# Six blocks of 384 tokens in place of one of 256 and four of 512, in a linear-attention, SwiGLU and ELU kernel

## The chip, the cores and the metric

The kernel runs on one core of one Trainium2 chip. The metric is the device time of one execution in microseconds (us). A change counts as faster or slower when it moves the time by more than 0.2%, which is about what a measurement of this kernel can tell from no change.

Four compute engines matter here: TensorE (PE in the rows; PEld is its loading of weights), VectorE (DVE), ScalarE (ACT) and GpSimd (POOL). SyncE (SP) issues the DMAs.

## The reference

Shapes: four batches, 8 heads, 576 positions, head size 64, hence 2304 tokens of model size 512; hidden sizes 1536 and 2048. The weights are float64, everything else float32.

```python
kv = np.einsum('bhsd,bhse->bhde', k, v)
out = np.einsum('bhsd,bhde->bhse', q, kv)
x = out / np.sqrt(np.mean(out * out, axis=-1, keepdims=True) + 1e-06) * g_norm
# heads side by side: x is [2304, 512]
xn = x / np.sqrt(np.mean(x * x, axis=-1, keepdims=True) + 1e-06) * rms_g
g = xn @ w_gate
x = g * (1.0 / (1.0 + np.exp(-g))) * (xn @ w_val) @ w_out
h = x @ w_in2
y = np.where(h > 0.0, h, np.exp(np.minimum(h, 0.0)) - 1.0) @ w_out2
```

## The kernel before

The 2304 tokens are 18 tiles of 128. The attention part goes by tiles: `sum_kv` makes a batch's k-by-v sums on TensorE, `attend` multiplies a tile's q with them (tile `po`), `norm` does the two norms on DVE, ACT and POOL (tiles `x`, `ms`, `me`, `ri`), and `turn` transposes the tile on TensorE (tile `pt`) and splits it exactly into two float32r parts, `xh` (copy on ACT) and `xl` (subtraction on DVE).

From there the work goes by **token blocks**. A block's tokens are the moving operand of the big products; `blocks` holds one of two tiles (256 tokens, block 0) and four of four tiles (512 tokens). x lies transposed, with the model dimension on the partitions, as two parts `xh` and `xl` for each block. Each weight chunk of 128x128 is also kept as two parts (`h...`, `l...`), and a product of weight and x is three matmuls, lines 240 to 242: high by high, high part of the weight by low part of x, low part of the weight by high part of x. So each 128x128 piece of a weight is used in three matmuls per block, whatever the block's size, and the moving operand has 512 or 256 columns.

The hidden dimension goes in chunks of 128, two chunks to a **group** (`G = 2`). There are six groups in the first phase (`hidden1`: gate `pg`, value `pv`, SiLU, product) and eight in the second (`hidden2`: `ph`, ELU). For one block in a group of the first phase, TensorE runs 48 matmuls for the two chunks' `pg` and `pv` and 24 for `back` (`pb`, the product with the output weights, added on DVE to the block's sums `acc`, line 298): 72. In the second phase it is 24 for `ph` and 24 for `back`: 48. After each block's hidden products the loop runs the `back` of the block before it, and then `bring`, which loads and splits one weight of the next group (float64 to two float32r parts, lines 224 to 235, on DVE and ACT, in the first group with POOL's help). Block 0 brings none, blocks 1 to 3 bring one each, and the last block of the turn brings what is left: three of six in the first phase, one of four in the second.

At the start the loads of k, v and the first of q go to places that later belong to the sums and to later blocks' x (`homes`). Then come the first block's attention, the second block's, the first block's first products, and from there the attention of the other tiles runs ahead of the products of the first group, as `until_turned` says. The program's lines give priorities; a scheduler sets the order on each engine when the kernel is built, and the engines then run that order, each waiting for the others by semaphores. In the last group the blocks go 1, 2, 3, 4, 0, so block 0 is also the last to be written out.

Of the kernel before, what the change touches and what calls it, by code (L numbers as in the profile page):

```python
# [18 lines left out]
G = 2  # hidden chunks that one pass over the tokens takes  # L19
EPS = 1e-06  # L20
INF_FIELD = 2.0**-96 * 1.875  # as bits: float64's infinity of float32, its exponent rebiased
# [3 lines left out]
def linear_attention__swiglu__elu_kernel(  # L25
    ctx: ExitStack,
    tc: tile.TileContext,
    q: bass.AP,  # [two token tiles, head pair's dim, tile, pair, token]
    kv: bass.AP,  # [token tile, token, k or v, model dim]
    g_norm: bass.AP,  # [1, D]  # L30
    w_gate: bass.AP,  # float64: [hidden chunk, model dim in chunk, chunk, hidden dim]
    w_val: bass.AP,
    w_out: bass.AP,  # float64: [hidden chunk, hidden dim, model dim]
    rms_g: bass.AP,  # [1, model dim]
    w_in2: bass.AP,
    w_out2: bass.AP,
    out: bass.AP,  # [model dim in chunk, chunk, token]
# [9 lines left out]
    # token blocks: the moving operand of the products  # L47
    blocks = []
    at = 0
    while at < NT:  # L50
        n = min(4, NT - at) if at else (NT % 4 or 4)
        blocks.append((at, n))
        at += n
    NMAX = 4 * P
    block_of = {i: (t, i - a) for t, (a, n) in enumerate(blocks) for i in range(a, a + n)}

    # per partition: x as two parts 72 KiB, the sums 36, the weights as two parts 40, the rest below 8 to 16 each
# [26 lines left out]
    kv_sb = {}  # L84
    kv_blocks = [const.tile([P, KD, P], F32, name=f"kv{j}") for j in range(3)]
    for t in kv_blocks:
        nc.gpsimd.memset(t, 0.0)  # off the diagonal it stays zero: a head's q meets its own kv alone
    in_sb, q_sb = {}, {}
    # k, v and the first of q wait where the sums, and later blocks' x, will lie
    homes = {}  # L90
    for tag, n, what in (
# [3 lines left out]
    ):  # L95
        for j, x in enumerate(what):
            homes[x] = tag, n, j
# [14 lines left out]
    def sum_kv(b):  # L112
# [3 lines left out]
        for i in tiles:  # L116
            r0, r1 = max(lo - i * P, 0), min(hi - i * P, P)
            for p in range(KD):
                # one zeroing of the bank: the pairs' sums lie side by side in it
# [26 lines left out]
    def attend(i):  # L146
        """q @ kv of a token tile, and each head's 1/rms"""
# [21 lines left out]
    def norm(i):  # L169
        """the two norms of a token tile"""  # L170
# [18 lines left out]
    def new_x(t):  # L189
        n = blocks[t][1] * P  # L190
        xh[t] = res.tile([P, KD, n], F32R, tag=f"xh{t}", name=f"xh{t}")
        xl[t] = res.tile([P, KD, n], F32R, tag=f"xl{t}", name=f"xl{t}")
# [19 lines left out]
    def split(src, kind, name, bufs, other=None):  # L212
# [9 lines left out]
        # the high word's exponent from bias 1023 to 127 (as a float, its exponent counts eights),  # L222
        # at most infinity's, then sign, exponent and 20 bits into a float32's places
# [4 lines left out]
        # plus the low word at its weight, rounded once to float32  # L228
# [56 lines left out]
    def back(ws, acts, t, first, last, name, done):  # L285
        """acts @ ws onto the block's sums"""
# [26 lines left out]
    def units(phase, g):  # L313
        """A group's weights: calls that load and split one each, in the order of need."""
# [26 lines left out]
    # The loads, in the order of need. The first block's x waits for all of its batch's k and v.  # L341
# [14 lines left out]
    load_kv(3)  # L356

    # The first block, the second one's attention, the other batches' kv; GpSimd takes a share of
    # the weights' passes while the vector engine has the tokens' as well.
    coming = [coming[i] for i in (0, 1, 3, 4, 2, 5)]  # L360
    bring(2)
    sum_kv(0)
# [99 lines left out]
```

## Time and profile before

| | |
|---|---|
| device time, median of 3 | 922.0 us (921.58 to 922.02) |
| span of the profiled execution | 920.5 us |
| PE busy | 894.7 us, 97% of the span |
| DVE busy | 641.0 us, 70% |
| ACT busy | 309.6 us, 34% |
| POOL busy | 86.9 us, 9% |

The profiled execution gives its span, from the first to the last instruction; the median lies 1.5 us above it, for what lies around the span. Busy time of PE is a share of time in which a matmul is under way; matmuls overlap one another, so the distance from one start to the next is what a matmul costs on a full engine, and this is read from the timeline.

### The profile page before, as it was taken

Reading aid. Unit: us, or ns where it says so; the run is one execution under the profiler, and the core shown is the slowest. Engines: PE = TensorE matmul, PEld = TensorE weight load, DVE = VectorE, ACT = ScalarE, POOL = GpSimd, SP = SyncE. Lnnn points to the kernel's source line nnn. Section 1 sums busy time; section 2 is a strip of 40 time slices with the busy share of each in tenths; the row PEclk is TensorE's granted clock in tenths of the full one; section 3 lists DMA queues with packets and bytes.
Section 4 is the critical chain, followed back from the end, with each engine's and each line's share of the span. In section 5 each row is a group of like instructions: output and inputs, shape, how many; then the busy total and the mean of one; then the engine's idle time right before and its main releaser. Section 6 shows DMA issues by size and latency. Waiting matters only on the chain.

```text
span 920.5 us, 11272 instructions
## 1 busy us (share of the span) xinstructions
PE 894.7 (97%) x4472; PEld 760.4 (83%) x4472; DVE 641.0 (70%) x1162; ACT 309.6 (34%) x563; POOL 86.9 (9%) x104
## 2 busy tenths in 40 slices
PE   5799999999999999999999999999999999999998
PEld 5787788888888888888888888888888888888886
DVE  4979846558557556665776775787878787878644
ACT  1345543222212221221233565433433433433332
POOL 1757723000000000000000000000000000000000
PEclk9899999999999999999999999999999999999999
DMA  9812201012002010210210011110101110100023
GB/s 336 352 58 90 69 23 69 23 47 69 23 24 69 33 36 23 69 46 24 69 40 29 24 46 46 47 46 23 68 24 46 46 47 24 69 23 1 0 92 115
DMA packets 16725, 55.55 MB, mean 60 GB/s; under 512 B 1872, under 2 KB 2384, under 8 KB 16672
## 3 DMA queue, kind: packets, MB, share of 16 engines
q1 hardware_dynamic: 16560, 54.53, 16.5%
q8 instruction: 35, 0.57, 0.2%
q0 software_dynamic: 112, 0.30, 0.2%
q14 instruction: 18, 0.15, 0.1%
HBM read 50.10 MB, written 4.72 MB: 60 GB/s over the span
## 4 chain that ended last, share of the span: by engine, by line
PE 89%; DVE 4%; POOL 4%; issue 1%; DMA 1%; ACT 0%; SPq 0%; DVEq 0%; POOLq 0%
PE pb L240 12%; PE pb L241 12%; PE pb L242 12%; PE ph L241 7%; PE ph L242 7%; PE ph L240 7%; PE pg L240 5%; PE pg L241 5%; PE pg L242 5%; PE pv L240 5%; PE pv L242 5%; PE pv L241 5%; POOL ri L166 1%; DMA wxh<-in_kv 1%; PE kv L120 1%
## 5 line engine op out<-in xcount | busy, mean ns | idle before, releaser
L298 DVE TENSOR_TENSOR acc<-acc,pb 128x512 f32<-128x512 f32 (+1 forms) x240 | 146.9, 628 | 27.4 <-PE pb L242 25.7
L255 ACT ACTIVATE ah<-a 128x512 fp32r<-128x512 f32 (+1 forms) x140 | 82.4, 588 | 247.4 <-PE pb L242 115.6
L241 PE MATMUL ph<-xl,hi 128*128 128x512 f32 (+1 forms) x320 | 117.8, 368 | 0.0
L240 PE MATMUL ph<-xh,hi 128*128 128x512 f32 (+1 forms) x320 | 117.7, 368 | 0.0
L242 PE MATMUL ph<-xh,li 128*128 128x512 f32 (+1 forms) x320 | 117.7, 368 | 0.0
L269 DVE TENSOR_TENSOR a<-s,pv 128x512 f32<-128x512 f32 (+1 forms) x60 | 37.9, 632 | 113.9 <-PE pv L242 111.7
L241 PE MATMUL pb<-al,hp 128*128 128x512 f32 (+1 forms) x320 | 116.6, 368 | 0.0
L242 PE MATMUL pb<-ah,lp 128*128 128x512 f32 (+1 forms) x320 | 116.6, 368 | 0.0
L240 PE MATMUL pb<-ah,hp 128*128 128x512 f32 (+1 forms) x320 | 113.7, 368 | 0.0
L256 DVE TENSOR_TENSOR al<-a,ah 128x512 fp32r<-128x512 f32 (+1 forms) x140 | 90.1, 644 | 32.9 <-ACT ah L255 32.3
L240 PE MATMUL pg<-xh,hg 128*128 128x512 f32 (+1 forms) x240 | 88.7, 370 | 1.5 <-ACT xh L203 1.5
L241 PE MATMUL pg<-xl,hg 128*128 128x512 f32 (+1 forms) x240 | 88.8, 370 | 0.5 <-DVE xl L204 0.5
L240 PE MATMUL pv<-xh,hv 128*128 128x512 f32 (+1 forms) x240 | 88.5, 369 | 0.5 <-ACT hv L233 0.5
L241 PE MATMUL pb<-al,ho 128*128 128x512 f32 (+1 forms) x240 | 88.7, 370 | 0.0
L242 PE MATMUL pg<-xh,lg 128*128 128x512 f32 (+1 forms) x240 | 88.4, 368 | 0.2 <-POOL lg L235 0.2
L241 PE MATMUL pv<-xl,hv 128*128 128x512 f32 (+1 forms) x240 | 88.4, 368 | 0.0
L242 PE MATMUL pv<-xh,lv 128*128 128x512 f32 (+1 forms) x240 | 88.3, 368 | 0.0
L242 PE MATMUL pb<-ah,lo 128*128 128x512 f32 (+1 forms) x240 | 88.0, 370 | 0.0
L240 PE MATMUL pb<-ah,ho 128*128 128x512 f32 (+1 forms) x240 | 85.3, 372 | 0.0
L280 DVE SCALAR_TENSOR_TENSOR a<-e,ph 128x512 f32<-128x512 f32 (+1 forms) x80 | 50.4, 631 | 46.9 <-ACT e L278 46.8
L277 ACT ACTIVATE e<-ph 128x512 f32<-128x512 f32 (+1 forms) x80 | 44.3, 554 | 77.0 <-PE ph L242 74.8
L240 PEld LDWEIGHTS ph<-xh,hi 128*128 128x128 f32 x320 | 60.4, 189 | 10.2
(111 smaller groups left out, 1474.2 us busy)
## 6 DMA issues: line engine op xcount, KB each, us to landing
ri<-in_w_in SPq DMA_DIRECT2D x16, 512.0 KB, 3.2
rp<-in_w_out SPq DMA_DIRECT2D x16, 512.0 KB, 3.2
rg<-in_w_gate SPq DMA_DIRECT2D x12, 512.0 KB, 3.3
rv<-in_w_val SPq DMA_DIRECT2D x12, 512.0 KB, 3.3
ro<-in_w_out SPq DMA_DIRECT2D x12, 512.0 KB, 4.2
out<-acc SPq DMA_DIRECT2D x16, 256.0 KB, 2.0
wacc<-in_kv SPq DMA_DIRECT2D x7, 512.0 KB, 10.2
wxh<-in_kv SPq DMA_DIRECT2D x6, 512.0 KB, 11.6
```

The costliest lines, as they stand in the source:

```text
L120: nc.tensor.matmul(acc[:, p, :], in_sb[i][r0:r1, p * P:(p + 1) * P], in_sb[i][r0:r1, DM + p * P:DM + (p + 1) * P], start=(i == tiles[0] an ...
L166: nc.gpsimd.tensor_tensor(ri, me, nhalf, op=ALU.pow)
L240: nc.tensor.matmul(acc, wh[:, s], mh, start=first, stop=False)
L241: nc.tensor.matmul(acc, wh[:, s], ml, start=False, stop=False)
L242: nc.tensor.matmul(acc, wl[:, s], mh, start=False, stop=last)
L255: nc.scalar.activation(h, a, AF.Copy)
L256: nc.vector.tensor_tensor(l, a, h.bitcast(F32), op=ALU.subtract)
L269: nc.vector.tensor_tensor(a, s, pv, op=ALU.mult)
L277: nc.scalar.activation(e, ph, AF.Relu, scale=-1.0)
L280: nc.vector.scalar_tensor_tensor(a, e, -1.0, ph, op0=ALU.add, op1=ALU.max)
L298: nc.vector.tensor_tensor(acc[:, e, :], acc[:, e, :], po, op=ALU.add)
```

## The change

`blocks` becomes six blocks of three tiles, 384 tokens each. `NMAX`, the width of the activation tiles, follows. A block's `xh` and `xl` become two halves of one tile `x0` to `x5`. The early k, v and q tiles get other homes to fit. The first block's attention is written for three tiles in place of two. Comments are dropped. Nothing in the lines of the products, the activations or the splitting of weights is changed, and the loops are the same; the loop over blocks has six turns in place of five, of which five bring a weight in place of four.

```diff
-    blocks = []
-    at = 0
-    while at < NT:
-        n = min(4, NT - at) if at else (NT % 4 or 4)
-        blocks.append((at, n))
-        at += n
-    NMAX = 4 * P
+    B = 3
+    blocks = [(at, min(B, NT - at)) for at in range(0, NT, B)]
+    NMAX = B * P
...
     homes = {}
-    for tag, n, what in (
-        ("xh2", 2, [0, 1]), ("xl2", 2, [2, 3]), ("acc0", 1, [4]), ("acc1", 2, [5, 6]), ("acc2", 2, [7, 8]),
-        ("acc3", 2, ["q1", "q2"]), ("acc4", 2, [9, 14]), ("xh3", 2, [10, 11]), ("xl3", 2, [12, "q0"]),
-        ("xh4", 2, [13, 15]), ("xl4", 2, [16, 17]),
+    for tag, what in (
+        ("x1", [0, 1, 2]), ("acc0", [3]), ("acc1", [4]), ("x2", [5, 6, 7]), ("acc2", [8]), ("acc3", ["q0"]),
+        ("acc4", [9]), ("x3", ["q1", 10, 11]), ("x4", ["q2", 12, 13]), ("x5", [14, 15, 16]), ("acc5", [17]),
     ):
         for j, x in enumerate(what):
-            homes[x] = tag, n, j
+            homes[x] = tag, len(what), j
...
     def new_x(t):
         n = blocks[t][1] * P
-        xh[t] = res.tile([P, KD, n], F32R, tag=f"xh{t}", name=f"xh{t}")
-        xl[t] = res.tile([P, KD, n], F32R, tag=f"xl{t}", name=f"xl{t}")
+        x = res.tile([P, 2, KD, n], F32R, tag=f"x{t}", name=f"x{t}")
+        xh[t], xl[t] = x[:, 0], x[:, 1]
...
-    attend(0)
-    attend(1)
+    first = range(blocks[0][1])
+    for i in first:
+        attend(i)
     bring(1, nc.gpsimd)
-    norm(0)
-    norm(1)
+    for i in first:
+        norm(i)
     bring(1, nc.gpsimd)
     sum_kv(1)
-    turn(0)
-    turn(1)
+    for i in first:
+        turn(i)
```

Three places show what the scheduler makes of it. Names end in a buffer's number; the digits before it are phase or chunk and block, so `pb0_0_0_0` is phase 0, group at chunk 0, block 0, first quarter of the model dimension.

**TensorE around the end of block 0's first products.** Here is the last of the 48 hidden matmuls of block 0 (`pv0_1_0`), then the k-by-v sums of batches 2 and 3, the transposes of the second block's tiles and the first `back`. Before:

```order
L242 MATMUL pv0_1_0_466<-xh0_285,lv1_260 128x256
L120 MATMUL kv2_487<-wxh3_132 128x128 x6
...
L120 MATMUL kv3_510<-wxl4_140 128x128 x4
L201 MATMUL pt3_542<-ident_82,x3_328 128x128 x4
L201 MATMUL pt4_549<-ident_82,x4_354 128x128 x4
L201 MATMUL pt5_556<-ident_82,x5_376 128x128 x4
L240 MATMUL pb0_0_0_0_564<-ah0_0_0_449,ho0_402 128x256
```

And now:

```order
L237 MATMUL pv0_1_0_472<-x0_307,lv1_282 128x384
L115 MATMUL kv2_493<-wacc4_131 128x128 x2
...
L115 MATMUL kv3_516<-wacc5_141 128x128 x4
L196 MATMUL pt3_540<-ident_82,x3_334 128x128 x4
L196 MATMUL pt4_547<-ident_82,x4_360 128x128 x4
L196 MATMUL pt5_554<-ident_82,x5_382 128x128 x4
L235 MATMUL pb0_0_0_0_562<-ah0_0_0_455,ho0_408 128x384
```

The order is the same, with 48 matmuls of 384 columns ahead of the sums where 48 of 256 stood, and tiles 0 to 5 are still all turned before the first `back`.

**TensorE at the start of block 2's products.** The rows run from the last hidden product of block 1 to the first matmul of block 2 that reads the low part of x. Before:

```order
L242 MATMUL pv0_1_1_892<-xh1_533,lv1_260 128x512
L201 MATMUL pt6_681<-ident_82,x6_603 128x128 x4
L155 MATMUL po10_690<-kv2_93,q5_688 128x128 x4
...
L201 MATMUL pt8_741<-ident_82,x8_640 128x128 x4
L155 MATMUL po12_750<-kv2_93,q6_748 128x128 x4
L201 MATMUL pt9_772<-ident_82,x9_662 128x128 x4
L240 MATMUL pg0_0_2_1068<-xh2_679,hg0_152 128x512
...
L241 MATMUL pg0_0_2_1068<-xl2_680,hg0_152 128x512
```

And now:

```order
L237 MATMUL pv0_1_1_857<-x1_539,lv1_282 128x384
L196 MATMUL pt6_678<-ident_82,x6_601 128x128 x4
L150 MATMUL po10_687<-kv2_93,q5_685 128x128 x4
...
L196 MATMUL pt8_738<-ident_82,x8_638 128x128 x4
L150 MATMUL po12_747<-kv2_93,q6_745 128x128 x4
L235 MATMUL pg0_0_2_1018<-x2_677,hg0_152 128x384
...
L196 MATMUL pt9_770<-ident_82,x9_660 128x128 x4
...
L236 MATMUL pg0_0_2_1018<-x2_677,hg0_152 128x384
```

Block 2 begins after tiles 6 to 8 in place of 6 to 9, and between block 1's products and block 2's stands the same attention work.

**VectorE at the end of the first group.** The splitting of the second group's last weights (`g3`, `v3`, `o3`) stands between the activations (`a`, `al`) of the last blocks. Before:

```order
L256 TENSOR_TENSOR al0_0_4_1345<-a0_0_4_1342,ah0_0_4_1344 128x512
L224 TENSOR_SCALAR cg3_1384<-rg3_1382 128x512
L224 TENSOR_SCALAR cv3_1399<-rv3_1397 128x512
L225 TENSOR_SCALAR cg3_1384<-cg3_1384 128x512
...
L269 TENSOR_TENSOR a0_1_4_1376<-s0_1_4_1374,pv0_1_4_1361 128x512
L227 SCALAR_TENSOR_TENSOR wg3_1385<-rg3_1382,cg3_1384 128x512
L227 SCALAR_TENSOR_TENSOR wv3_1400<-rv3_1397,cv3_1399 128x512
L224 TENSOR_SCALAR co3_1414<-ro3_1412 128x512
```

And now:

```order
L251 TENSOR_TENSOR al0_0_4_1341<-a0_0_4_1338,ah0_0_4_1340 128x384
L219 TENSOR_SCALAR cg3_1380<-rg3_1378 128x512
...
L222 SCALAR_TENSOR_TENSOR wg3_1381<-rg3_1378,cg3_1380 128x512
L251 TENSOR_TENSOR al0_1_4_1375<-a0_1_4_1372,ah0_1_4_1374 128x384
...
L225 SCALAR_TENSOR_TENSOR cg3_1380<-rg3_1378,cg3_1380 128x512
L264 TENSOR_TENSOR a0_0_5_1454<-s0_0_5_1452,pv0_0_5_1439 128x384
L251 TENSOR_TENSOR al0_0_5_1457<-a0_0_5_1454,ah0_0_5_1456 128x384
L219 TENSOR_SCALAR cv3_1496<-rv3_1494 128x512
```

`g3` is now split during block 4 alone, and `v3` and `o3` a block later; before, all three fell into the last block.

## Rows read from the trace of the kernel before

**Rows 1.** From the page: busy time and share of the span; then the 40 slices of the span, each digit the busy share in tenths.

```profile
span 920.5 us, 11272 instructions
PE 894.7 (97%) x4472; PEld 760.4 (83%) x4472; DVE 641.0 (70%) x1162; ACT 309.6 (34%) x563; POOL 86.9 (9%) x104
...
PE   5799999999999999999999999999999999999998
...
DVE  4979846558557556665776775787878787878644
```

**Rows 2.** The stretches view of the steady part: length, busy time (and instructions) of PE, PEld, DVE, ACT and POOL, granted clock, DMA share, GB/s.

```profile
160.00:900.00 740.00, 740.00 (x3568) 625.53 (x3567) 514.09 (x948) 241.26 (x426) 0.00 (x0) 1.00 0.12 40
```

**Rows 3.** The groups view of PE with shapes kept apart: the first and the last of the fifteen groups of 512 columns and of the fifteen of 256 columns of lines 240 to 242, with counts.

```profile
L240 PE MATMUL ph<-xh,hi 128*128 128x512 f32 x256 | 99.7, 389 | 0.0
...
L240 PE MATMUL pb<-ah,ho 128*128 128x512 f32 x192 | 71.6, 391 | 0.0
L242 PE MATMUL ph<-xh,li 128*128 128x256 f32 x64 | 18.1, 283 | 0.0
...
L242 PE MATMUL pb<-ah,lo 128*128 128x256 f32 x48 | 13.2, 291 | 0.0
```

**Rows 4.** The timeline of PE in the steady part: start, length, line, tiles, shape. A run of 512 columns, a run of 256 columns, and a 512 run that turns to 256.

```profile
440.20 0.39 PE L242 MATMUL pb<-ah,lo 128*128 128x512 f32 x1
...
441.56 0.39 PE L242 MATMUL pb<-ah,lo 128*128 128x512 f32 x1
...
442.50 0.28 PE L240 MATMUL pg<-xh,hg 128*128 128x256 f32 x1
...
443.94 0.28 PE L240 MATMUL pv<-xh,hv 128*128 128x256 f32 x1
...
448.31 0.28 PE L240 MATMUL pg<-xh,hg 128*128 128x256 f32 x1
448.42 0.28 PE L241 MATMUL pg<-xl,hg 128*128 128x256 f32 x1
448.54 0.40 PE L241 MATMUL pb<-al,ho 128*128 128x512 f32 x1
```

**Rows 5.** The chain that ended last, in order of time: start, length, what. The pieces at the same place of one group and the next, in the first and in the second phase.

```profile
223.45 0.47 PE pb L240 x2
...
297.47 0.47 PE pb L240 x2
...
618.17 0.47 PE pb L240 x2
...
667.49 0.47 PE pb L240 x2
```

**Rows 6.** The stretches view of the start, columns as in rows 2.

```profile
19.00:37.30 18.30, 12.56 (x89) 11.61 (x89) 15.87 (x28) 6.07 (x12) 11.06 (x12) 0.81 1.03 409
37.30:59.20 21.90, 19.68 (x161) 18.32 (x160) 20.72 (x34) 9.46 (x20) 19.23 (x21) 0.98 0.36 138
59.20:86.40 27.20, 26.07 (x164) 22.82 (x163) 21.75 (x38) 13.50 (x28) 14.91 (x21) 0.96 0.18 59
86.40:160.00 73.60, 71.56 (x365) 59.97 (x364) 50.37 (x83) 33.32 (x67) 38.33 (x40) 1.00 0.19 65
```

**Rows 7.** The timeline of PE: the last transpose before the first `back`, and the starts of blocks 2 and 3, with idle time before and what ended it in brackets.

```profile
58.28 1.11 PE L201 MATMUL pt<-ident,x 128*128 128x128 f32 x4 [1.47 <-DVE x L184]
...
83.89 0.50 PE L240 MATMUL pg<-xh,hg 128*128 128x512 f32 x1 [0.69 <-ACT xh L203]
...
86.47 0.50 PE L241 MATMUL pg<-xl,hg 128*128 128x512 f32 x1
...
108.92 0.50 PE L240 MATMUL pg<-xh,hg 128*128 128x512 f32 x1 [0.79 <-ACT xh L203]
```

**Rows 8.** The timeline of POOL: idle places between the first norms and the saturated stretch, and the last norm of the second block.

```profile
27.02 0.19 POOL L181 TENSOR_SCALAR me<-ms 128x1 f32<-128x1 f32 x1 [1.15 <-ACT po L179]
...
34.08 1.27 POOL L231 TENSOR_TENSOR wv<-wv,cv 128x512 f32<-128x512 f32 x1 [1.23 <-DVE cv L230]
36.67 1.28 POOL L235 TENSOR_TENSOR lv<-wv,hv 128x512 fp32r<-128x512 f32 x1 [1.32 <-ACT hv L233]
...
55.51 0.93 POOL L183 TENSOR_TENSOR ri<-me,nhalf 128x1 f32<-128x1 f32 x1
```

**Rows 9.** The timeline of PE at the change from the first group to the second.

```profile
152.94 0.28 PE L241 MATMUL pg<-xl,hg 128*128 128x256 f32 x1
153.75 0.39 PE L240 MATMUL pv<-xh,hv 128*128 128x256 f32 x1 [0.53 <-ACT hv L233]
153.97 0.28 PE L241 MATMUL pv<-xl,hv 128*128 128x256 f32 x1
154.44 0.38 PE L242 MATMUL pg<-xh,lg 128*128 128x256 f32 x1 [0.19 <-POOL lg L235]
154.66 0.28 PE L240 MATMUL pg<-xh,hg 128*128 128x256 f32 x1
```

**Rows 10.** The timeline of DVE at the end: two additions of 512 columns in a row, and the four of the last block. Then one group of the second phase as a stretch, columns as in rows 2.

```profile
909.93 1.28 DVE L298 TENSOR_TENSOR acc<-acc,pb 128x512 f32<-128x512 f32 x2 [0.82 <-PE pb L242]
...
915.25 1.41 DVE L298 TENSOR_TENSOR acc<-acc,pb 128x256 f32<-128x256 f32 x4 [1.36 <-PE pb L242]
...
600.00:649.30 49.30, 49.30 (x242) 41.78 (x241) 38.77 (x73) 19.10 (x34) 0.00 (x0) 1.00 0.13 43
```

## The prediction

> **What bounds the kernel now.** I read the page first: TensorE is busy 97% of the span, and its slices are at nine tenths or more from the third on [rows 1]. DVE comes second with 70%, near full only at the start. The stretches view then says where TensorE waits: from 160 to 900 us it is busy 740.00 of 740.00 us, at the full granted clock, 2.4 GHz [rows 2]. So over four fifths of the span the time is the number of matmuls times the distance between two starts, and nothing that DVE, ACT or the DMAs do there is on the path. TensorE's idle time lies ahead of 160 us, where the attention keeps DVE and POOL busy: 5.7 us of the 18.3 to 37.3 us, 2.2 of the next 21.9, 1.1 of the next 27.2, 2.0 of the 73.6 up to 160 [rows 6].
>
> The distance is read from the timeline [rows 4]. Six steps of 512 columns take 441.56 - 440.20 = 1.36 us, 0.2267 each. Twelve steps of 256 columns take 443.94 - 442.50 = 1.44 us, 0.1200 each. The lengths in the groups view, 0.389 and 0.283 [rows 3], are of matmuls that overlap, and aren't used.
>
> **What the change does to TensorE's steady work.** Of 512 columns there are 6 x 256 + 9 x 192 = 3264 matmuls, of 256 columns 6 x 64 + 9 x 48 = 816 [rows 3]: each piece of a weight part is used in four of the one and one of the other. Now it is used in six of 384 columns, 816 x 6 = 4896. The columns are the same 2304 per piece, so what changes is the number of matmuls, six in place of five. What a matmul costs besides its columns follows from the two distances: 256 more columns cost 0.1067 us, so 256 columns carry 0.1200 - 0.1067 = 0.0133 us besides. That is the same as 0.2267 - 2 x 0.1067. On that line 384 columns cost 0.0133 + 0.1600 = 0.1733 us.
>
> The check is the length of a group in the chain. By the two distances it should be 288 x 0.2267 + 72 x 0.1200 = 73.9 us in the first phase and 192 x 0.2267 + 48 x 0.1200 = 49.3 us in the second. A group of the first phase, 4 x 72 matmuls of 512 and 72 of 256, takes 297.47 - 223.45 = 74.02 us; one of the second, 4 x 48 and 48, takes 667.49 - 618.17 = 49.32 us [rows 5]. Now they hold 6 x 72 = 432 and 6 x 48 = 288 matmuls of 0.1733: 74.88 and 49.92 us. That is 0.86 us more in each of six groups and 0.60 in each of eight: 5.2 + 4.8 = **+10.0 us**.
>
> 384 columns stand nowhere in this trace. The bounds by price per column are 0.2267 x 384 / 512 = 0.1700 and 0.1200 x 384 / 256 = 0.1800. I take the line, 0.1733: with it one number, 0.0133, explains both neighbours, while either bound makes one of them wrong.
>
> The Trainium skill, page "TensorE: Matmul & The Clock Gate", section "Back-to-back issue gap", gives a distance of the columns at 2.4 GHz and about 2.5 ns besides. This trace doesn't agree: it shows 13.3 ns besides, at both sizes. By the page's figure the 816 added matmuls would cost an estimated 2.0 us in place of 10.0 or so.
>
> **The start.** Part of the ten microseconds falls where TensorE waits anyhow. The order rows show that the two sequences are the same up to block 2: tiles 0 to 5 turned, then the first `back`, then block 1, then tiles 6 to 8 turned. What ends TensorE's waits there is the norms: tile 5 by DVE at 58.3 us, behind POOL's power at 55.5 to 56.4, and x of block 2, whose low part releases the first products at 86.47 [rows 7, 8]. The number of tiles ahead of each point, and what DVE and POOL do for them, hardly changes: one tile's norms move from the second block to the first, and three turned tiles in place of four release block 2. So I let block 2's products begin at 86.5 us as before. By then TensorE has done 72 matmuls of 256 and 48 of 512 columns, 8.6 + 10.9 = 19.5 us; now 120 of 384, 20.8 us. The 1.3 us more lie in the idle 2.2 us of 37.3 to 59.2 [rows 6], which cover the 48 x 0.0533 = 2.6 us that block 0's hidden products grow by, while block 1's shrink by as much and the wait ahead of block 2 grows. Term: **-1.3 us**.
>
> At the change to the second group, TensorE's first matmuls wait for the high part of `v3` and the low part of `g3`: from 152.94 to 154.66 us, 1.72 us, stand four steps that at 0.12 would be 0.48 [rows 9]. The order rows show why: three weights, `g3`, `v3` and `o3`, were split in the last block. Now `g3` is split a block earlier, 72 x 0.1733 = 12.5 us, and two are left. Term: **-1.2 us**. If `v3` is still late, half of it stays.
>
> The wait at the start of block 3, 0.79 us and what follows it [rows 7], I leave as it is: less hidden work (48 x 0.1733 = 8.3 us in place of 10.9) stands between two blocks, but one tile less is needed.
>
> **The other engines.** An operation of DVE costs less per instruction when narrower, but not in proportion: 512 columns follow each other at 1.28 - 0.68 = 0.60 us, with 0.68 the length of one, and four of 256 take 1.41 us, 0.33 each after the first [rows 10]. 384 then is 0.47, and per operation type 6 x 0.47 in place of 4 x 0.60 + 0.33, 0.07 us more per set. With 8 such sets in each of 14 groups (four of `acc`, two of `a`, two of `al`) that is 112 x 0.07 = 8 us of DVE work in 740 in which TensorE never waited for it, so nothing. At the end the four last additions are of 384 columns in place of 256: 4 x 0.14 = 0.56 us, of which the last six matmuls, slower by 6 x 0.0533 = 0.32, cover about half: **+0.3 us**.
>
> The homes: the order on SyncE's queue has the same loads in the same places, each to a fresh place, so they start as before; places are given back by the k-by-v sums long before x needs them. One tile for `xh` and `xl` adds no wait between engines in the order, since `xl` reads `xh` and follows it anyhow. Both at zero; were either wrong, the price is a wait of one copy, 0.6 us, per tile turned, 18 x 0.6 = 11 us at the very most, all ahead of 130 us.
>
> **Sum.** 10.0 - 1.3 - 1.2 + 0.3 = +7.8 us. The profiled span of 920.5 becomes 928.3; with the 1.5 us by which the median lies above it, **929.8 us**, 0.85% slower.
>
> **Rivals.**
>
> *A: the matmul of 384 columns costs its share of one of 512.* Then the 0.120 of 256 columns is a floor of another kind (the next weight's loading, say), and the rest is 0.443 ns a column. For it: the first step of 256 columns after a run of 512 is 448.42 - 448.31 = 0.11 us, not 0.12 [rows 4], as if a lead were being used up. Against it: one fixed part explains both steady distances to the last digit. Price: 0.1700 x 6 - (4 x 0.2267 + 0.1200) = -0.0067 us per piece, x 816 = -5.4 us; with -0.9 at the start in place of -1.3, and the other two terms, -7.2 us: 914.8 us. It turns the sign as soon as 384 columns cost under 0.1733 - 7.8 / 4896 = 0.1717 us. Chance 0.07.
>
> *B: the added matmuls cost nothing besides their columns.* The 13 ns would then be tied to something that doesn't grow with the number of matmuls. The first term goes, and the rest is -2.2 us: 919.8 us, at the edge of what can be measured. Both steady distances speak against it [rows 4]. Chance 0.02. The Trainium skill's 2.5 ns, named above, points this way; with its estimated 2.0 us the time would be some 921.8 us.
>
> *C: the start gives back more.* POOL has 1.15 + 1.23 + 1.32 us of idle time between 26 and 37 us [rows 8], while the second block's norms are behind it later. With a third tile's small operations drawn into these places, tile 5 is ready some 3 to 4 us sooner, and what follows moves up with it. Against it: DVE is at 20.7 of 21.9 us there [rows 6], and its work ahead of tile 5 doesn't shrink. Price: a further -3.7 us: 926.1. Chance 0.13.
>
> *D: DVE becomes the bound of single turns in the second phase.* A group's DVE work was 38.8 us [rows 10], of which 4 x 8 x 0.60 + 8 x 0.33 = 21.9 us were activations and additions, so a weight's splitting takes 16.9 / 4 = 4.2 us. A turn of 384 columns with one weight is then 8 x 0.47 + 4.2 = 8.0 us of DVE against 48 x 0.1733 = 8.3 of TensorE, 96%, where it was 9.0 of 10.9. Four such turns follow each other in a group, then two with 3.8 us. For it: hardly any slack for an order that isn't ideal. Against it: over the group it is 39 of 50 us, and the products of a block have a block's time before their `back` needs them. Price: 0.25 us in each of 8 x 4 turns, +8 us: 937.8. Chance 0.13.
>
> **How the numbers follow.** The forecast as it stands, 927 to 932.5 us with what the waits of the start may do, has 0.61; A 0.07, B 0.02, C 0.13, D 0.13; 0.04 for what I haven't thought of. The range takes in the forecast, C and the nearer half of D: 925 to 935 us; it leaves out A, B, the far half of D and the rest, under 0.2. Faster by over 0.2% (under 920.2 us) is A and half of B: 0.08. Within 0.2% is the other half of B and the far end of C: 0.05. Slower by more: 0.87. Measurements of this kernel can tell about 0.2% from no change.
>
> **What will show it.** In the timeline, the distance of 384 columns in a run: 0.1733 us if I am right, 0.170 under A. In the chain, groups of 74.9 and 49.9 us; longer ones, with idle time of TensorE between 160 and 900 us, mean D. The first matmul of block 2 that reads the low part at about 86 us; at 82 or 83 C is right. The waits at the change to the second group gone or halved. I am wrong altogether if the matmuls of 384 columns come at an uneven distance, or if TensorE waits in the steady part.

## The result, and the profile after

The changed kernel takes **933.87 us** (median of 4 runs, 933.69 to 934.33), the kernel before 921.79 us on the same chip (4 runs, 921.48 to 922.02). The ratio is 1.0131 with a 95% interval of 1.0117 to 1.0145: 1.3% slower, or 10.8 to 13.4 us. The profiled span went from 920.5 to 931.9 us.

First the page of the changed kernel, against [rows 1]: span, busy time and counts, and the slices.

```profile
span 931.9 us, 13167 instructions
...
PE 903.1 (97%) x5288; PEld 898.3 (96%) x5288; DVE 653.5 (70%) x1270; ACT 324.8 (35%) x647; POOL 86.4 (9%) x104
...
PE   5698899999999999999999999999999999999998
...
PEclk9799999999999999999999999999999999999999
```

TensorE has 816 records more, as the change has it, and is at 97% again. VectorE has 12.5 us more to do and is still at 70%.

Then the stretches view of the changed kernel, the steady part and the four pieces of the start, against [rows 2, 6]. Columns: length, busy time (and instructions) of PE, PEld, DVE, ACT and POOL, granted clock, DMA share, GB/s.

```profile
160.00:900.00 740.00, 740.00 (x4271) 740.00 (x4270) 521.86 (x1042) 249.88 (x493) 0.00 (x0) 1.00 0.12 40
19.00:37.30 18.30, 9.49 (x67) 8.06 (x65) 16.73 (x29) 6.05 (x13) 13.36 (x15) 0.76 1.03 409
37.30:59.20 21.90, 21.73 (x148) 21.12 (x149) 19.57 (x32) 8.92 (x18) 16.32 (x17) 0.89 0.35 134
59.20:86.40 27.20, 25.18 (x177) 23.91 (x175) 19.55 (x35) 13.88 (x30) 14.01 (x18) 1.00 0.17 59
86.40:160.00 73.60, 70.61 (x427) 69.99 (x428) 52.25 (x90) 34.59 (x74) 39.34 (x43) 0.98 0.19 65
```

The steady part looks as before: TensorE never waits, at full clock. In the start, the first piece has lost 3.1 us of TensorE's work (9.49 us, 12.56 before), and in the second TensorE is busy nearly throughout, but at a granted clock of 0.89.

The distance of 384 columns is read from the timeline of the changed kernel (start, length, line, tiles, shape), the group from its chain (start, length, what): the same place in one group and the next, in the first phase and in the second, as in [rows 4, 5].

```profile
440.58 0.33 PE L235 MATMUL pg<-x,hg 128*128 128x384 f32 x1
...
442.14 0.33 PE L235 MATMUL pg<-x,hg 128*128 128x384 f32 x1
```

```profile
207.95 0.17 PE pb L236
...
282.83 0.17 PE pb L236
...
618.06 0.17 PE ph L235
...
667.98 0.17 PE ph L235
```

Nine steps take 442.14 - 440.58 = 1.56 us, 0.1733 each. The groups take 74.88 and 49.92 us. All three are the predicted numbers to the last digit shown, and 6 x (74.88 - 74.02) + 8 x (49.92 - 49.32) = 10.0 us is the steady term.

The rest of the 11.4 us is in the start. This is the timeline of PE there in the changed kernel; what stands in brackets is the idle time before and what ended it.

```profile
30.60 1.09 PE L196 MATMUL pt<-ident,x 128*128 128x128 f32 x4 [4.17 <-DVE x L179]
33.27 1.09 PE L196 MATMUL pt<-ident,x 128*128 128x128 f32 x4 [1.58 <-DVE x L179]
37.47 1.08 PE L196 MATMUL pt<-ident,x 128*128 128x128 f32 x4 [3.12 <-ACT hv L228]
38.35 5.46 PE L150 MATMUL po<-kv,wx 128*128 128x128 f32 x32
43.57 0.42 PE L235 MATMUL pg<-x,hg 128*128 128x384 f32 x1
...
62.22 0.42 PE L235 MATMUL pb<-ah,ho 128*128 128x384 f32 x1
...
88.36 0.44 PE L236 MATMUL pg<-x,hg 128*128 128x384 f32 x1
...
98.99 0.63 PE L196 MATMUL pt<-ident,x 128*128 128x128 f32 x4 [2.54 <-DVE x L179]
```

The first `back` and the turn of tile 10 in the timeline of PE before:

```profile
59.22 0.58 PE L240 MATMUL pb<-ah,ho 128*128 128x256 f32 x1
...
96.81 0.60 PE L201 MATMUL pt<-ident,x 128*128 128x128 f32 x4
```

And the last pass of VectorE over x of tile 10, first before, then in the changed kernel:

```profile
95.58 0.75 DVE L184 SCALAR_TENSOR_TENSOR x<-x,ri,rg_sb 128x512 f32<-128x512 f32 x1 [0.98 <-POOL ri L183]
```

```profile
98.11 0.74 DVE L179 SCALAR_TENSOR_TENSOR x<-x,ri,rg_sb 128x512 f32<-128x512 f32 x1
```

The first block now has a third tile to turn, its norms end later, and the 32 attention records of the second block stand behind that turn and ahead of the first products. Those begin at 43.57 us, where before they began at 37.28. Block 2's first low-part product is at 88.36 us, where before it was at 86.47 [rows 7]. Then comes a wait of 2.54 us for tile 10 that the kernel before doesn't have: there x of that tile was ready at 96.33 us (95.58 + 0.75) and its turn followed at 96.81 without a wait; now it is ready at 98.85, while the products ahead of the turn end near 96.3. The four steps at the change to the second group [rows 9] have lost their waits: no step there is over 0.15 us late.

So the ledger of the span is +10.0 (steady) - 1.25 (the wait at the second group) + 0.0 (the end: from the last matmul's start to the end 4.76 us, 4.82 before) and, as what is left of 11.4, **+2.65 for the start**. The prediction had -1.3 there.

Where these 2.65 us arise is seen when the matmuls done by a point, each at its full-clock distance, are taken from the time of that point in both traces. At the first `back` both kernels have done the same records, and the changed one is 3.0 us later, 2.6 of it the larger products of block 0: 0.4 us lost. At block 2's first low-part product it is 0.8 us. The other 1.9 us come behind it, at tile 10's turn and what follows it. The kernel before, whose products begin earlier, loses most of that lead again between its first products and its first `back`.

### The profile page after: what moved, and what is told of

Same layout as the page of the kernel before. It is cut to its first block, busy times and chain, and to the rows that moved or that the text cites. A ratio compares the mean times of both kernels' runs of the same rounds, so it can differ in the third digit from the quotient of the medians.

```text
span 931.9 us, 13167 instructions
## 1 busy us (share of the span) xinstructions
PE 903.1 (97%) x5288; PEld 898.3 (96%) x5288; DVE 653.5 (70%) x1270; ACT 324.8 (35%) x647; POOL 86.4 (9%) x104
## 4 chain that ended last, share of the span: by engine, by line
PE 93%; DVE 3%; POOL 2%; DMA 1%; issue 1%; ACT 0%; SPq 0%; DVEq 0%
PE pb L235 13%; PE pb L236 13%; PE pb L237 13%; PE ph L235 7%; PE ph L236 7%; PE ph L237 7%; PE pg L235 5%; PE pv L235 5%; PE pv L237 5%; PE pg L237 5%; PE pv L236 5%; PE pg L236 5%; PE kv L115 2%; POOL ri L161 1%; PE po L150 1%; DMA wx<-in_kv 1%
## 5 line engine op out<-in xcount | busy, mean ns | idle before, releaser
L293 DVE TENSOR_TENSOR acc<-acc,pb 128x384 f32<-128x384 f32 x288 | 157.1, 550 | 33.0 <-PE pb L237 31.2
L235 PE MATMUL ph<-x,hi 128*128 128x384 f32 x384 | 128.3, 334 | 0.0
L236 PE MATMUL ph<-x,hi 128*128 128x384 f32 x384 | 128.3, 334 | 0.0
L237 PE MATMUL ph<-x,li 128*128 128x384 f32 x384 | 128.3, 334 | 0.0
L236 PE MATMUL pb<-al,hp 128*128 128x384 f32 x384 | 125.4, 334 | 0.0
L237 PE MATMUL pb<-ah,lp 128*128 128x384 f32 x384 | 125.4, 334 | 0.0
L235 PE MATMUL pb<-ah,hp 128*128 128x384 f32 x384 | 123.9, 334 | 0.0
L237 PE MATMUL pb<-ah,lo 128*128 128x384 f32 x288 | 97.0, 337 | 0.0
L236 PE MATMUL pb<-al,ho 128*128 128x384 f32 x288 | 96.9, 336 | 0.0
L236 PE MATMUL pg<-x,hg 128*128 128x384 f32 x288 | 96.6, 335 | 0.0
L235 PE MATMUL pg<-x,hg 128*128 128x384 f32 x288 | 96.5, 335 | 0.0
L235 PE MATMUL pv<-x,hv 128*128 128x384 f32 x288 | 96.4, 335 | 0.0
L236 PE MATMUL pv<-x,hv 128*128 128x384 f32 x288 | 96.4, 335 | 0.0
L237 PE MATMUL pv<-x,lv 128*128 128x384 f32 x288 | 96.3, 334 | 0.0
## 6 DMA issues: line engine op xcount, KB each, us to landing
wx<-in_kv SPq DMA_DIRECT2D x13, 512.0 KB, 10.2
```

Of the source, the lines that this page charges most:

```text
L235: nc.tensor.matmul(acc, wh[:, s], mh, start=first, stop=False)
L236: nc.tensor.matmul(acc, wh[:, s], ml, start=False, stop=False)
L237: nc.tensor.matmul(acc, wl[:, s], mh, start=False, stop=last)
L293: nc.vector.tensor_tensor(acc[:, e, :], acc[:, e, :], po, op=ALU.add)
```

## The experiments

Theory 1 is the prediction's sum with the start as measured: 13.3 ns for each added matmul, and a start that got longer. On why it got longer there are 1a, that the first products come late, and 1b, that VectorE's norms of a later tile set the end of the start anyhow. All ratios are to the kernel before, run on the same chip.

**One tile for both parts of x, and homes in such tiles, without the new sizes.** The edit is to the changed kernel; the lines of the homes, fitted to the old sizes, are left out.

```
-    blocks = [(at, min(B, NT - at)) for at in range(0, NT, B)]
...
+    for n in (2, 4, 4, 4, 4):
+        blocks.append((sum(b[1] for b in blocks), n))
...
```

> The kernel before in its own block sizes (256, then four of 512), with the one part of the change that is not the size: a block's high and low parts of x in one tile, and the early k, v and q tiles re-homed to match. Theory 1 (the time comes from the sizes alone: 13.3 ns for each added matmul, and a start with three tiles in the first block): 921.8 us, no change within 0.5, and the first products at about 37 us as before. Rival (the shared tile or the new places hold up the start): up to the 2.5 us that the sum left unexplained, 924.3 us, with new waits before 110 us.

Measured: 0.9999 (0.9987 to 1.0011). First products at 37.10 us. The tile and homes in it cost nothing that can be measured; what is left is the sizes.

**Is it 13 ns for each matmul?** Two kernels from the one before, with the second phase's hidden products on 512 columns split into halves. The first runs the two halves one behind the other on the same weights; the second has the loop over the halves outermost, so that the weights change with every matmul.

```
-        into(ph, w, t)
+        if n == 4 * P:
+            for c in range(KD):
+                for part, (ws, xs) in enumerate(((w[0], xh[t]), (w[0], xl[t]), (w[1], xh[t]))):
+                    for half in range(2):
+                        s = slice(half * 2 * P, (half + 1) * 2 * P)
+                        nc.tensor.matmul(ph[:, s], ws[:, c * P:(c + 1) * P], xs[:, c, s], ...)
+        else:
+            into(ph, w, t)
```

> The kernel before, in which the second phase's first products on 512 columns are each done as two of 256 columns, one right behind the other on the same weights (768 matmuls more, the same columns, nothing else moved). Theory 1 (each matmul costs 13.3 ns besides its columns, whatever stands next to it): 768 x (2 x 0.1200 - 0.2267) = +10.2 us, 932.0 us, and a mean distance of 0.120 us between the halves. Rival A (a matmul on the weights that the one ahead of it used has no such cost, so the fixed part belongs to a change of weights): about 921.8 us, distances of 0.120 and 0.107 in turn. Rival B (the added matmuls cost much less than 13.3 ns each, and the change lost its 10 us elsewhere): 923 us or less.

> As the split of 512 columns into halves, with all twelve products of the first half ahead of the twelve of the second, so that the weights change with every matmul, as everywhere in the kernel before. Theory 1: again 768 x 0.0133 = +10.2 us, 932.0 us. If the fixed part belongs to a change of weights, this one shows +10.2 us and the other order shows none; if it belongs to every matmul, both show it.

Measured: 1.0117 (1.0102 to 1.0132) and 1.0109 (1.0094 to 1.0124), +10.8 and +10.1 us. Both show the 10.2 us. In the timeline of the first (two halves to a row), pairs follow each other at 0.24 us:

```profile
699.74 0.40 PE L280 MATMUL ph<-xh,hi 128*128 128x256 f32 x2
...
701.18 0.40 PE L280 MATMUL ph<-xh,hi 128*128 128x256 f32 x2
```

Six pairs take 1.44 us, so 0.120 each matmul, the number for 256 columns with other weights each time. Both pages have 5240 weight loads, one for each matmul: weights that are used twice in a row are loaded twice. So whether the 13.3 ns belong to the matmul or to its load isn't separated. That added matmuls are free (rival B of the prediction) is refuted. By the 2.5 ns besides the columns that the Trainium skill gives for a matmul taken by itself, without the load of its weights ("TensorE: Matmul & The Clock Gate", "Back-to-back issue gap"), an estimated 1.9 us would have been seen; these runs don't agree with it.

**Nine blocks of 256.**

```
-    B = 3
+    B = 2
...
```

> The changed kernel with nine blocks of 256 tokens: 816 matmuls for each block, all of 256 columns. Theory 1 (0.120 us each, so 13.3 ns besides the columns): 9 x 816 x 0.1200 = 881.3 us of products against 838.7 in before, +42.6; with nothing else changed 921.8 + 42.6 = 964.4 us, and 960 to 967 as the start has a first block of two tiles and the turns for the weights are more. Rival A (the fixed part is not constant but grows as the tile shrinks, since loading 128 weight columns then covers a larger part of a matmul): over 967 us, a distance over 0.120. Rival B (VectorE or ScalarE becomes the bound, with more and smaller passes): over 975 us and waits of TensorE throughout.

With these blocks the fourth batch's sums overwrite the first's before tile 4 has read them; the work and its order are otherwise the same. Measured: 1.0422 (1.0406 to 1.0438), +38.9 us. The distance is 0.120 throughout and TensorE has no wait after 160 us, so neither rival holds. The first block has two tiles again, and TensorE's idle and slow time before 120 us, summed over the steps of its timeline, is 21.3 us against 23.9 in before: 42.6 - 2.6, and the 1.25 us of the second group, give 38.8.

**What in the sizes costs the start?** First two blocks as in the change, the others of 512, so that the steady part is that of before.

```
-    blocks = [(at, min(B, NT - at)) for at in range(0, NT, B)]
...
+    for n in (3, 3, 4, 4, 4):
+        blocks.append((sum(b[1] for b in blocks), n))
...
```

> The changed kernel with block sizes of 3, 3, 4, 4 and 4 tiles (384, 384, 512, 512, 512). It has the first two blocks of the change and as many matmuls, of the same mean size, as the kernel before: 2 x 0.1733 + 3 x 0.2267 = 0.120 + 4 x 0.2267 = 1.027 us for each place in the program, so the steady part is that of before, and only the start differs. Theory 1a (the first block of three tiles costs the start; its products begin at 43.6 us and the rest only follows): 921.8 + 2.5 = 924.3 us. Theory 1b (up to 80 us the idle time of TensorE differs by only 0.9 us between the two traces, the rest is lost at 80 to 120 us, where a third block of three tiles leaves too few products to cover VectorE's norms of tile 10): about 921.8 + 0.9 = 922.7 us, and no wait of 2.5 us near 99 us. Rival (512 columns beside 384 ones save nothing, the cost sits in the number of blocks): 931 us or more.

Measured: 1.0033 (1.0022 to 1.0044), +3.0 us (2.0 to 4.1). First products at 43.66 us, 32 attention records ahead of them, as in the changed kernel. The wait at the second group is gone here too, and changes between 512 and 384 columns cost some 2.0 us more than those between 512 and 256 did in before: the steps behind 120 us are together 2.9 us above 0.2267 and 0.1733 each, against 0.9 without the wait in before, and behind 160 us, where TensorE never waits, all that is above lies in the eight steps that follow a change of size. With 1.25 less and 2.0 more, some 2.2 of the 3.0 us are the start's; in the profiled execution, whose span is 3.6 us longer than before's, it is 2.8. So three-tile first blocks make the start as much longer as in the changed kernel, and 1b, by which 0.9 us were to be expected, fails by its size. Its wait near 99 us is indeed gone, but with a third block of four tiles TensorE loses more at tile 9's turn, where the changed kernel waits 0.77 and 0.54 us:

```profile
85.73 0.66 PE L197 MATMUL pt<-ident,x 128*128 128x128 f32 x4 [1.30 <-DVE x L200]
86.92 2.87 PE L151 MATMUL po<-kv,q 128*64 128x128 f32 x16 [0.53 <-DVE x L200]
```

From 86.97 to 90.38 us its granted clock is 0.50. So in these two executions the size of the third block moves the loss and doesn't remove it.

**Undoing the late start in the changed kernel, by two ways.** The first moves a split of weights behind the turns:

```
-    bring(1, nc.gpsimd)
     sum_kv(1)
     for i in first:
         turn(i)
+    bring(1, nc.gpsimd)
```

> The changed kernel with the split of the second value weight v1 written behind the turning of the first block's tiles, not ahead of the second batch's sum. In the trace of the changed kernel the turning of tile 2 waits 3.1 us, put down to ScalarE's part of such a split, at 37.5 us. Theory 1a (the late first products cost the end): they begin 2 to 4 us sooner than 43.6 us, and the time falls by as much, to 930 to 932 us. Theory 1b (VectorE's work up to the norms of tile 10 sets when TensorE is free of waits, and moving its passes about saves nothing): the products begin sooner, the wait near 99 us grows by as much, 933.9 us within 0.5.

Measured: 1.0113 (1.0098 to 1.0128), which isn't told apart from the changed kernel. The wait of 3.11 us stays, and the products begin at 43.14 us. The trace shows why: on every engine the same instructions stand in the same order as in the changed kernel. The scheduler put the split back where it was, so this run tests neither 1a nor 1b; it is a second measurement of the changed kernel. The wait need not be the split's either. In the changed kernel VectorE's last pass over x of tile 2 ends at 37.32 us, 0.15 us ahead of the turn that waited, as it does at the turns of tiles 0 and 1, so the norm alone explains it:

```profile
36.29 1.03 DVE L179 SCALAR_TENSOR_TENSOR x<-x,ri,rg_sb 128x512 f32<-128x512 f32 x1
```

The second writes the second block's attention between the first block's turns:

```
     for i in first:
         turn(i)
-    for i in second:
-        attend(i)
+        attend(i + len(first))
+    for i in second:
         norm(i)
```

> The changed kernel with the attention of the second block's tiles written between the turns of the first block's (turn 0, attention 3, turn 1, attention 4, turn 2, attention 5), and their norms behind them: TensorE does these 32 records, 5.46 us in the trace of the changed kernel, inside its waits of 4.2, 1.6 and 3.1 us rather than behind them. Theory 1a: the first products begin 3 to 5 us sooner than 43.6 us, and the time falls by 2 to 3 us, to 931 to 932 us. Theory 1b: VectorE's norms of tile 10 end no sooner, so the wait near 99 us takes up what was gained: 933.9 us within 0.5.

Measured: 1.0059 (1.0047 to 1.0071). That is 6.6 us less than the 1.0131 of the changed kernel and 5.0 less than its second measurement, about twice what 1a allowed. The timeline of PE of this kernel:

```profile
31.06 1.09 PE L196 MATMUL pt<-ident,x 128*128 128x128 f32 x4 [3.82 <-DVE x L179]
31.94 1.92 PE L150 MATMUL po<-kv,wx 128*128 128x128 f32 x8
33.73 1.08 PE L196 MATMUL pt<-ident,x 128*128 128x128 f32 x4
34.74 2.00 PE L150 MATMUL po<-kv,wx 128*64 128x128 f32 x16
37.93 0.63 PE L196 MATMUL pt<-ident,x 128*128 128x128 f32 x4 [1.19 <-DVE x L179]
...
41.40 0.42 PE L235 MATMUL pg<-x,hg 128*128 128x384 f32 x1
...
58.07 0.42 PE L235 MATMUL pb<-ah,ho 128*128 128x384 f32 x1
...
94.83 0.63 PE L196 MATMUL pt<-ident,x 128*128 128x128 f32 x4 [2.54 <-DVE x L179]
```

The attention fills two of the three waits, and the third batch's sums go ahead of the products as well. The clock has its part in it; first the changed kernel, then this one, by stretches:

```profile
33.00:36.00 3.00, 1.09 (x4) 0.72 (x4) 2.92 (x6) 0.60 (x1) 2.38 (x3) 0.50 1.03 407
36.00:39.00 3.00, 1.53 (x8) 1.56 (x9) 3.00 (x4) 1.03 (x2) 2.04 (x2) 0.50 1.03 408
39.00:42.00 3.00, 3.00 (x18) 2.77 (x18) 2.93 (x7) 0.79 (x2) 0.13 (x1) 0.50 0.93 371
```

```profile
33.00:36.00 3.00, 3.00 (x19) 2.53 (x19) 2.95 (x5) 1.52 (x3) 2.32 (x3) 0.55 1.03 408
36.00:39.00 3.00, 1.81 (x20) 1.60 (x17) 2.97 (x6) 1.52 (x3) 1.69 (x3) 1.00 1.03 410
39.00:42.00 3.00, 3.00 (x26) 2.89 (x25) 3.00 (x6) 0.79 (x2) 2.92 (x3) 1.00 0.96 381
```

In the changed kernel TensorE ran at 0.50 (1.2 GHz) from its waits near 30 us to 42 us, most of the attention records among it; here it is at full clock from about 36 us. The wait for tile 10 didn't grow, as by 1b it would have: it is 2.54 us in both, and 4.16 us earlier here. The attention that leads to that tile stands on TensorE behind the first products, so it moves up with them. The first `back` moves by 4.15 us (58.07 for 62.22). Of the 5.7 us by which the profiled span is shorter, the other 1.6 are the half clock behind tile 10's turn, which the changed kernel's trace has and this one doesn't.

**The attention behind the first products.**

```
-    for i in second:
-        attend(i)
-        norm(i)
...
     acts = [hidden1((ready[f"g{j}"], ready[f"v{j}"]), 0, f"0_{j}_0") for j in range(G)]
     sum_kv(2)
     sum_kv(3)
+    for i in second:
+        attend(i)
+        norm(i)
```

> The changed kernel with the second block's attention and norms written behind the first block's products and the sums of the last two batches, so that none of its 32 records stands ahead of the first products, and none fills the waits ahead of them either. Theory 1a, order: the products begin 2 to 3 us sooner than 43.6 us and the time falls by 2 to 3 us, 931 to 932 us. Theory 1a, clock: TensorE is as idle before 39 us as in the changed kernel, so its clock comes back no sooner than 42 us and the first products run at half clock; together with them less than 2 us are won. Rival (VectorE): the norms of tiles 3 to 5 begin later than in the changed kernel, TensorE waits for them behind the first block's products, and the time is 934 to 940 us.

Here the fourth batch's sums overwrite the first's before tiles 3 and 4 have read them; the instructions are the same. Measured: 1.0230 (1.0216 to 1.0245), 942.97 us, slower as the rival had it and by more than its 934 to 940 us:

```profile
69.53 0.87 PE L196 MATMUL pt<-ident,x 128*128 128x128 f32 x3 [6.81 <-DVE x L179]
```

The attention out of the way gave nothing, since the third batch's sums took its place ahead of the products (43.05 us), and the norms that follow the attention came late. So 1a isn't the whole either: the second block's attention must be early enough for its norms. (Since it reads what the fourth batch's sums have overwritten, it also waits 1.04 us for their copy, at 58.99 us; behind the products but ahead of those sums it was not tried.)

**The wait at the second group, alone, in the kernel before.**

```
-    bring(len(coming) if t == turns[-1] else 1, ...)
+    bring(len(coming) if t == turns[-1] else 2 if k == 0 and t == turns[-2] else 1, ...)
```

> The kernel before, with one edit: in the first group of hidden chunks the last two blocks prepare two and two of the next group's weights, not one and three. In the trace of before, TensorE waits 0.56 and 0.70 us at the change to the second group for the weights g3 and v3, the last prepared; the changed kernel, with one turn more, has no such wait. Theory 1: the 1.25 us are this wait and nothing else, so 921.8 - 1.2 = 920.6 us, without the wait in the trace. Rival (the wait only moves, to the block ahead, where VectorE has the norms as well): 921.8 us.

Measured: 0.9982 (0.9972 to 0.9991), 1.7 us faster (0.8 to 2.6), and no wait behind 120 us in the trace. The gain rests on the ten times: the profiled execution, the slowest of them, has a span of 920.5 us as before, since its start is 1.2 us longer. It is the fastest kernel of this study.

**Together, in the kernel before and with its number of matmuls.** The attention is written between the turns, and the weights are spread as above. The first of three:

```
-    turn(0)
-    turn(1)
...
+    for i in (0, 1):
+        turn(i)
+        attend(second[i])
     for i in second:
-        attend(i)
+        if i > 3:
+            attend(i)
         norm(i)
```

> The kernel before with two edits that the runs so far point to: two and two weights in the last turns of the first group (as in the run with that edit alone, 1.7 us faster), and the attention of tiles 2 and 3 written behind the turns of tiles 0 and 1, so that four of its records fill TensorE's longest wait. Theory 1a (in the start what counts is when the first products begin, and at which granted clock): the start of before has already little ahead of its first products (37.3 us), so at most 1 to 2 us more, 918.5 to 920.5 us. Rival (the norms set the start, and only the spread weights count): 920.5 us.

> As the kernel before with both edits, but with all the attention of tiles 2 to 5 in pairs behind the two turns, none left behind the first products. Theory 1a: twelve records more in the wait ahead of the second turn, a granted clock back at full some us sooner than 34.3 us, but four records more ahead of the first products: 918 to 920.5 us. Rival (the norms set the start): 920.5 us.

> Blocks of 3, 3, 4, 4 and 4 tiles, as many matmuls as before, with the attention between the turns and two and two weights in the last turns of the first group. Theory 1a with what the runs measured: 925.7 (this kernel without the two edits) - 5.2 (what the attention between the turns gave in the changed kernel) - 1.9 (the spread weights) = 918.6 us, 917 to 920. Rival (the gain in the changed kernel hung on its third block of three tiles): 922 to 924 us.

Measured: 1.0028 (1.0019 to 1.0037), 1.0040 (1.0026 to 1.0053) and 0.9993 (0.9984 to 1.0002). None does what was expected. In the first of them, TensorE waits for tile 7 where the kernel before didn't, and its clock falls to 0.50 from 79.77 to 86.60 us (timeline of PE, then the stretch):

```profile
67.61 2.84 PE L155 MATMUL po<-kv,q 128*128 128x128 f32 x24
...
81.55 1.08 PE L201 MATMUL pt<-ident,x 128*128 128x128 f32 x4 [4.97 <-DVE x L184]
```

```profile
80.00:100.00 20.00, 17.34 (x92) 14.62 (x93) 19.03 (x29) 10.27 (x22) 18.51 (x23) 0.84 0.23 79
```

Tile 7 belongs to the third block, which the edit doesn't name. Before, the attention of its four tiles stands in one piece behind three of block 1's hidden products; here only the first tile's does, and that of the other three stands behind 27 of them, at 67.61 us, so their norms can only begin later. The row before:

```profile
63.94 3.74 PE L155 MATMUL po<-kv,q 128*128 128x128 f32 x32
```

The second kernel shows the same, with a wait of 4.85 us for tile 7. Why the scheduler parted that attention isn't shown, nor what the edit would have given without it. The third is 3.7 us better than the same sizes without the edits. The expectation had counted the spread weights twice: with a first block of three tiles there is no wait at the second group to take away.

## Why the prediction was right, and where not

**The steady term, +10.0 us: right.** Distance, groups and the even run are as predicted, and the split and the nine blocks show the same 13.3 ns in other places. Rival A (0.1700) and rival B are refuted by the timeline, rival D by 740.00 busy us of 740.00.

**The wait at the second group, -1.2 us: right**, 1.25, and shown by itself in the kernel before.

**The end, +0.3 us: 0.0.** The four last additions took 1.95 us for 1.41 [rows 10], as counted, but from their end to that of the span it is 3.5 us where it was 3.8.

**The homes and the tile, zero: right** in the run with one tile and new homes for the old sizes; the changed kernel's own homes were not run without its sizes.

**The start, -1.3 us: wrong in sign, +2.65 us measured.** Two steps failed, each with about half of the 4.0 us.

The first is "So I let block 2's products begin at 86.5 us as before", with its reason that the number of tiles ahead of each point "hardly changes". They came 1.9 us late. The order rows that it rests on begin at the end of block 0's products; ahead of them one tile did change its place: the third one's norms and turn came ahead of the first products, and the second block's attention stood behind that turn on TensorE. The idle 2.2 us that were to cover block 0's growth were indeed used up (0.17 us are left between 37.3 and 59.2; the stretch before, 18.3 us long, begins at 19.0 us and not at 18.3 as the prediction has it), but by products that began 6.3 us later than in before (43.57 and 37.28 us by the timelines), the records ahead of them at half clock. So the growth of block 0 showed in full: 3.0 us at the first `back`, and 0.8 us lost in place of 1.3 gained at block 2. That this delay is handed on shows where the attention was moved between the turns: the first `back` and tile 10's turn both moved by some 4.15 us.

The second is "The wait at the start of block 3, 0.79 us and what follows it [rows 7], I leave as it is", with its reason that less hidden work stands between two blocks but "one tile less is needed". The less work counted and the tile less didn't: tile 10's x was ready 2.5 us later than before (98.85 and 96.33 us), the 8.3 us of products that stand ahead of its turn were through near 96.3, and TensorE waited 2.54 us and then ran 3.41 us at half clock. This is the other 1.9 us. The clock makes much of it: the second measurement of the same order of instructions has the wait without the half clock, and its profiled span is 2.0 us shorter.

Rival C (a start that gives more back) went the wrong way as well.

**VectorE, no cost: right.** Its added work was put at 8 us (the 0.07 us a set is 0.09 by the rounded numbers beside it); in the 740 us it is 7.8, 521.86 for 514.09, and TensorE waits for none of it.

The total lies inside the range, 1.1 us from its upper edge, because an error of 4.0 us in one term stands beside 10.0 that were right; the sign and the steady term were worked out, the place inside the range is luck. By how much the late products and by how much the half clock ahead of them made the start longer isn't settled: the run that mended the one mended the other.

## What to carry to other kernels

When TensorE is full, count its matmuls and measure the distance at two sizes; the line through both gave a third size to the last digit. For the start, a step that moves one tile ahead of a point must be followed through TensorE's own order from the first instruction, since what is queued behind its wait moves too, and at whichever clock the wait leaves; and smaller blocks leave less work to cover a wait for a later tile. An edit that repairs a start in one tiling (attention between the turns: 5 to 7 us less) can go with a longer one in another (+2.6 us, together with the spread weights), so it is to be measured anew in each, and the trace says first whether the scheduler has kept the order that the lines were to give.

## What the runs showed of the chip that was not expected

At a granted clock of 0.50 the fixed part isn't seen: 384 columns follow each other there at 0.32 us, 384 / 1.2 GHz, and at 0.1733 us at full clock. These rows are from the changed kernel, behind the wait for tile 10:

```profile
100.71 0.52 PE L235 MATMUL pb<-ah,ho 128*128 128x384 f32 x1
101.03 0.52 PE L236 MATMUL pb<-al,ho 128*128 128x384 f32 x1
...
103.81 0.34 PE L236 MATMUL pb<-al,ho 128*128 128x384 f32 x1
103.99 0.34 PE L237 MATMUL pb<-ah,lo 128*128 128x384 f32 x1
```

And the same wait doesn't always cost the clock. The changed kernel waits 2.54 us for tile 10 and then runs 3.41 us at 0.50; the run with the later split, whose engines execute the same instructions in the same order, waits 2.55 us at the same place and stays at full clock. Over these 3.41 us, first the changed kernel, then the other:

```profile
100.26:103.67 3.41, 3.41 (x13) 3.41 (x12) 3.41 (x6) 1.47 (x4) 1.55 (x2) 0.50 0.00 0
```

```profile
100.26:103.67 3.41, 3.41 (x23) 3.41 (x22) 3.33 (x7) 2.29 (x6) 1.53 (x2) 1.00 0.00 0
```

That is half of 3.41, 1.7 us, the greater part of the 2.0 us by which the second one's profiled span is shorter (929.9), and its other runs go up to 933.7 us. A single profiled execution of these kernels therefore can't tell a microsecond or two; the intervals over several runs can.
